# Linear attention with a routed MoE: order pinned in all wide tiles, weights in two transfers, a last turn over two PSUM tiles

## The chip, the cores and the metric

One core of a Trainium2 chip. The time is that of one execution on the device in microseconds; a median of three runs is given. Engines: PE (matmul), PEld (its weight loads), DVE, ACT, POOL, and SP, which only issues transfers.

## What is computed

Decayed linear attention over 4 batches, 8 heads, 768 positions, width 64, in blocks with a state that is carried on; its output as 3072 tokens of 512 goes through a mixture of eight experts, one per token:

```python
intra = einsum('bhij,bhjd->bhid', einsum('bhic,bhjc->bhij', qb, kb) * Dmask, vb)
inter = einsum('bhid,bhde->bhie', qb * lam_pow, kv_state)
out   = intra + inter
kv_state = lam_block * kv_state + einsum('bhsd,bhse->bhde', kb * rev_pow, vb)
...
logits = x @ w_gate + modality_bias[modality_id]
e_idx  = argmax(logits, axis=1)              # gate_w: its softmax weight
for e in range(8):
    out[e_idx == e] = gate_w * (relu(x @ w1[e]) @ w2[e])
```

## The kernel before

Attention runs over 24 blocks of 128 positions (`g`), two at a time in 12 pairs (`j`, the loop at L851). Per pair: scores on PE, masks on DVE, outputs from the state and from the masked scores on PE, a copy to `xt` on ACT. One pair later each block is turned into token rows together with its logits by `tokens`, in two halves (L291 to L300): PE writes PSUM, ACT copies to `xn`, and after the second half ACT's queue stores 128 rows to `xs` in device memory. The last pair has no later pair to hide in; its turn stands at L904 to L910, with a PSUM tile `xp` for each block whose halves it uses one after the other.

After every sixth block the tokens of a batch are routed (`route`, `ranks`, `places`), and one indirect write for each block fills a table `inv` (POOL) that lists tokens by expert; the last twelve come after attention, between the matmuls of tile 0. The MoE works through tiles of tokens of one expert: two wide tiles of 256 tokens from an early list (made from the first two batches, `early_list`, L439), two thin tiles (64 and 32 tokens), then ten or more wide ones from a late list (`late_list`). In this run 12 wide tiles are done and no conditional one.

A wide tile splits float32 operands into a high and a low part (`split`, L546: ACT casts `hi`, DVE subtracts for `lo`) and takes three matmuls for each product (`three`). The first layer (`wide`, L621) has four quarters of 24 matmuls of 256 columns; quarters 0 and 2 share one PSUM tile, 1 and 3 the other. After each quarter ACT makes `hh`, DVE makes `hl` (L632, L633) and `tail` splits a quarter of w2. Then the gathered rows of the next tile are transposed (`turn_rows`, L606), and the second layer (`second`) takes 48 matmuls of 512 columns. The weights of the next tile (`raw1` to `w1h`, `w1l`) are split too, each quarter once PE has read the old one. POOL gathers rows (`fetch_rows`, L573) and scatters results (L699); SP loads indices and weights (`fetch_w1` L588, `fetch_w2` L594, four transfers of 512 KB each, left out by a condition where the expert stays).

The order on an engine comes from a scheduler, except where `pinned` ties an operation behind the one pinned last on its engine. Before the change only the first wide tile is pinned (`run`, L950, third argument of `wide`), and most steps of the lists aren't.

Of the kernel before, what the change touches and what calls it, by code (L numbers as in the profile page):

```python
# [6 lines left out]
F32 = mybir.dt.float32  # L7
# [33 lines left out]
def linear_attention_moe(tc, qkv, lam, modality, wg, mbias, w1, w2, out):  # L41
    nc = tc.nc
    with ExitStack() as ctx:
# [159 lines left out]
        copies, logits, ranked, fades = [], [], [], []  # L203
# [77 lines left out]
        def outputs(g, pt, op):  # L281
            vt, blk = loaded(g)[2], g % HB
            for p in range(NP):
                for hl in range(2):
                    mm = pinned(nc.tensor.matmul(op[blk][halves2[hl ^ blk], p, :], vt[:, (2 * p + hl) * D : (2 * p + hl + 1) * D],  # L285
                                                 pt[:, hl, p, :], start=(g % NC == 0 and p == 0), stop=(p == NP - 1)))
            xt = work.tile([P, NP, P], F32, name="xt", bufs=3)
            copies.append(pinned(nc.scalar.copy(out=xt, in_=op[blk])))
            return xt, mm

        def tokens(g, hf, xt, xn, xp):  # L291
# [5 lines left out]
            copies.append(pinned(nc.scalar.copy(out=xn[:, blk, 2 * hf : 2 * hf + 2, :], in_=xp[:, :, : P + E])))  # L297
# [97 lines left out]

        def count_tiles(first, nm):
# [8 lines left out]
            nc.vector.tensor_tensor(out=ge, in0=cnt.unsqueeze(2).to_broadcast([1, E, CAP // TT]), in1=ge, op=ALU.is_ge)  # L405
            nt = const.tile([1, E], F32, name="nt" + nm)
            nc.vector.tensor_reduce(out=nt, in_=ge, axis=AX, op=ALU.add)
            return cnt, nt

        def list_ends(num, nm):  # L410
# [4 lines left out]
            nc.vector.tensor_tensor(out=tmp, in0=tri[:, :g, :g], in1=num.unsqueeze(1).to_broadcast([1, g, g]), op=ALU.mult)  # L415
            nc.vector.tensor_reduce(out=ends, in_=tmp, axis=AX, op=ALU.add)
            return ends

        def tile_list(num, delta, base0, items, nm, ends=None):
# [6 lines left out]
            pinned(nc.vector.tensor_tensor(out=past, in0=sidx[:, :items].unsqueeze(2).to_broadcast(sh),  # L426
                                           in1=ends.unsqueeze(1).to_broadcast(sh), op=ALU.is_ge))
            ex = const.tile([1, items], F32, name="ex" + nm)
            nc.vector.tensor_reduce(out=ex, in_=past, axis=AX, op=ALU.add)
            nc.vector.tensor_tensor(out=past, in0=past, in1=delta.unsqueeze(1).to_broadcast(sh), op=ALU.mult)  # L430
            at = const.tile([1, items], F32, name="at" + nm)
            nc.vector.tensor_reduce(out=at, in_=past, axis=AX, op=ALU.add)
            nc.vector.tensor_tensor(out=at, in0=at, in1=sidx[:, :items], op=ALU.add)
            if base0 is not None:
                nc.vector.tensor_tensor(out=at, in0=at, in1=base0.to_broadcast([1, items]), op=ALU.add)
            nc.vector.tensor_scalar(out=at, in0=at, scalar1=float(EMPTY), scalar2=None, op0=ALU.min)
            return ends, ex, at

        def early_list():  # L439
            cnt, full = count_tiles(TT, "A")  # L440
            ends = list_ends(full, "A")
            yield
# [9 lines left out]

            took = const.tile([1, E, EARLY], F32, name="took")
# [5 lines left out]
            yield ex, nA  # L459

        def late_list(cnt, n2, exA, nA):
# [9 lines left out]
            def first_of(those, nm):  # L471
# [25 lines left out]
            nc.vector.tensor_copy(out=exs[:, 0:1], in_=exA[:, EARLY - 1 : EARLY])  # L497
            others = const.tile([1, LIST], F32, name="others")
            facts = const.tile([1, 3, E], F32, name="facts")
            nc.vector.tensor_tensor(out=facts[:, 0, :], in0=sidx[:, :E], in1=exA[:, EARLY - 1 : EARLY].to_broadcast([1, E]),  # L500
                                    op=ALU.subtract)
# [4 lines left out]
            nc.vector.tensor_copy(out=start[:, 0, :], in_=exA[:, EARLY - 1 : EARLY])  # L506
# [15 lines left out]
            nc.vector.tensor_tensor(out=base[:, :E], in0=ebase, in1=nA, op=ALU.add)  # L522
# [71 lines left out]
        def fetch_w2(er, kw, after=None):  # L594
            for i in range(4):
                ld = nc.sync.dma_start(out=raw2[i], in_=w2[bass.ds(er, 1), :, 2 * i : 2 * i + 2].rearrange("o p f n -> p (o f) n"), **kw)
                if after is not None:
                    behind(ld, after)

        def turn_rows(cols, before=None, part=range(2), pin=False):  # L600
            for i in part:
                tp = ps.tile([P, 2, TT], F32, name=("x", "kv")[i], bufs=1)
                for j in range(2):
                    kc = 2 * i + j
                    for t, m in groups(cols):
                        mm = nc.tensor.transpose(out=tp[:, j, t * P : t * P + m],  # L606
                                                 in_=xg[t][:m, kc * (P + E) : kc * (P + E) + P], identity=ident[:m, :m])
                        if before is not None:
                            behind(mm, before, wait=False)
                        if pin and before is None:  # L610
                            pinned(mm)
                split(tp[:, :, :cols], xh[i][:, :, :cols], xl[i][:, :, :cols], pin)
# [118 lines left out]
        def fetch_both(er, kw):  # L731

            first, second = parts(F32)
            for i in range(4):
                nc.sync.dma_start(out=first[i], in_=w1[bass.ds(er, 1), :, i].rearrange("o p k f -> p (o k) f"), **kw)
            second = [t.rearrange("p k f -> p (k f)").rearrange("p (f n) -> p f n", f=2) for t in second]
            for i in range(4):
                nc.sync.dma_start(out=second[i],
                                  in_=w2[bass.ds(er, 1), :, 2 * i : 2 * i + 2].rearrange("o p f n -> p (o f) n"), **kw)
            return first, second  # L740

        raw1 = [const.tile([P, KC, TT], F32, name=f"raw1{i}") for i in range(4)]
        raw2 = [const.tile([P, 2, DM], F32, name=f"raw2{i}") for i in range(4)]
# [5 lines left out]
        w1h, w1l = parts(F32R)  # L749
# [15 lines left out]
        nums = const.tile([1, 1], I32, name="nums")  # L765
        thr = const.tile([1, E, CAP // TT], F32, name="thr")
# [84 lines left out]
        for j in range(1, pairs):  # L851
# [9 lines left out]
            if j == early + 1:  # L861
                exA, nA = next(listing)
# [20 lines left out]
            if j == early:  # L883
                listing = early_list()
                next(listing)
# [89 lines left out]
        def run_early(n):  # L975
# [3 lines left out]
            whole = wide(tail)  # L979
# [16 lines left out]
            w1h, w1l = parts(F32R)  # L996
# [11 lines left out]
        pins.clear()  # L1008
# [60 lines left out]
```

## Time and profile before

| | us |
|---|---|
| median of three runs (430.03 to 431.52) | 431.52 |
| the profiled execution | 429.08 |
| its span, first to last instruction | 427.4 |
| PE busy | 402.7 |
| DVE busy | 246.1 |
| ACT busy | 182.6 |
| POOL busy | 107.4 |
| mean granted TensorE clock, share of full | 0.986 |

Stages by PE's first matmul of each: attention to 109.2, tile 0 from 116.94, tile 1 from 141.66, thin tiles from 164.6, late wide tiles from 180.11 to 414.6, then the last result and the end at 427.4. A matmul record lasts longer than the step to the next one, since matmuls overlap: 0.28 us a record and some 0.12 us a step in the first layer.

### The profile page before, as it was taken

To read this page: it belongs to the slowest core of one execution; us is meant where nothing else is said; L and a number is where in the kernel's file an instruction comes from. 1 tells how busy PE (TensorE), PEld (TensorE's weight loads), DVE (VectorE), ACT (ScalarE), POOL (GpSimd) and SP (SyncE) were. 2 spreads that over 40 slices of the span, in tenths; PEclk is the share of its full clock that TensorE was granted. 3 is DMA by queue.
4 is the path that set the end of the run, shared out by engine and by line. 5 is a ranking of instruction groups with operands and counts; after the bars stand their busy time and mean duration, and the time that the engine had idled before them with its cause. 6 is when DMAs were issued, how large, how long until landed. Compare 5 with 4: busy or idle time off the path is not lost.

```text
span 427.4 us, 9911 instructions
## 1 busy us (share of the span) xinstructions
PE 402.7 (94%) x3864; PEld 356.8 (84%) x3864; DVE 246.1 (58%) x431; ACT 182.6 (43%) x277; POOL 107.4 (25%) x116
## 2 busy tenths in 40 slices
PE   8799999999599999899999999999999999999980
PEld 4599999899498986698989999898989899998960
DVE  4568777888389740377563819193755638191600
ACT  1032323324466331465554637182635546381510
POOL 5010144262268531154020111101020201101010
PEclk9899999999999999999999999999999999999995
DMA  5999999996830128412036684302020111101000
GB/s 202 324 357 348 391 381 342 348 327 216 277 129 3 51 64 281 170 55 78 26 78 221 212 284 147 135 20 78 26 78 25 54 49 46 50 2 41 11 30 18
DMA packets 25655, 63.85 MB, mean 149 GB/s; under 512 B 7157, under 2 KB 8701, under 8 KB 25600
## 3 DMA queue, kind: packets, MB, share of 16 engines
q1 hardware_dynamic: 17360, 43.36, 29.3%
q0 software_dynamic: 4768, 13.08, 9.2%
q10 hardware_dynamic: 3472, 6.69, 4.1%
q8 instruction: 32, 0.52, 0.5%
q14 instruction: 23, 0.19, 0.1%
HBM read 91.40 MB, written 14.07 MB: 247 GB/s over the span
## 4 chain that ended last, share of the span: by engine, by line
issue 48%; PE 20%; DMA 12%; POOL 8%; DVE 6%; SPq 2%; ACT 1%; POOLq 0%; ACTq 0%; DVEq 0%
PE s L232 5%; PE x L296 5%; PE o L285 5%; POOL out_dram L699 4%; DMA idx<-inv 4%; POOL xg L573 3%; DMA xg<-xs,idx 3%; PE o L278 3%; PE kv L252 2%; SPq L590 1%; DMA xg<-xs,idxA 1%; DMA raw<-in_w_dram 1%; DVE w1l L548 1%; DMA dk<-tab_d 1%; DVE w2l L548 1%
## 5 line engine op out<-in xcount | busy, mean ns | idle before, releaser
L615 PE MATMUL s<-xh,w1h 128*128 128x256 f32 x384 | 109.4, 285 | 0.7
L619 PE MATMUL s<-xh,w1l 128*128 128x256 f32 x384 | 107.9, 281 | 0.4 <-DVE w1l L548 0.4
L618 PE MATMUL s<-xl,w1h 128*128 128x256 f32 x384 | 107.8, 281 | 0.0
L548 DVE TENSOR_TENSOR w1l<-raw,w1h 128x1024 fp32r<-128x1024 f32 x46 | 55.6, 1225 | 84.4 <-ACT w1h L547 84.4
L615 PE MATMUL o<-w2h,hh 128*128 128x512 f32 x192 | 75.8, 395 | 0.0
L615 PEld LDWEIGHTS s<-xh,w1h 128*128 128x128 f32 x384 | 72.3, 188 | 4.0 <-DVE hl L633 2.3
L618 PE MATMUL o<-w2l,hh 128*128 128x512 f32 x192 | 74.8, 390 | 0.0
L619 PE MATMUL o<-w2h,hl 128*128 128x512 f32 x192 | 74.8, 389 | 0.0
L619 PEld LDWEIGHTS s<-xh,w1l 128*128 128x128 f32 x384 | 72.4, 188 | 0.6 <-DVE w1l L548 0.6
L618 PEld LDWEIGHTS s<-xl,w1h 128*128 128x128 f32 x384 | 72.4, 188 | 0.4
L548 DVE TENSOR_TENSOR w2l<-raw,w2h 128x1024 fp32r<-128x1024 f32 x48 | 58.4, 1216 | 2.6 <-ACT w2h L547 2.4
L547 ACT CAST w1h<-raw 128x1024 fp32r<-128x1024 f32 x46 | 47.5, 1053 | 27.3 <-PE s L618 21.3
L547 ACT CAST w2h<-raw 128x1024 fp32r<-128x1024 f32 x48 | 49.9, 1039 | 0.0
L699 POOL DMA_INDIRECT out_dram<-y,idx x20 | 20.2, 1008 | 106.7 <-ACT y L698 106.7
L698 ACT ACTIVATE y<-o,idx 128x512 f32<-128x512 f32 x20 | 13.8, 690 | 77.2 <-PE o L619 44.3
L573 POOL DMA_INDIRECT xg<-xs,idx x20 | 25.0, 1251 | 86.0 <-PE kv L606 74.8
L619 PEld LDWEIGHTS o<-w2h,hl 128*128 128x128 f32 x192 | 36.0, 188 | 7.7
L615 PEld LDWEIGHTS o<-w2h,hh 128*128 128x128 f32 x192 | 36.1, 188 | 7.2
L618 PEld LDWEIGHTS o<-w2l,hh 128*128 128x128 f32 x192 | 36.1, 188 | 7.1
L633 DVE SCALAR_TENSOR_TENSOR hl<-s,hh 128x512 fp32r<-128x512 f32 x48 | 32.8, 683 | 16.0 <-ACT hh L632 15.8
L388 POOL DMA_INDIRECT inv<-pay,sloti x24 | 32.5, 1356 | 25.2 <-PE x L296 6.3
L632 ACT ACTIVATE hh<-s 128x512 fp32r<-128x512 f32 x48 | 28.6, 595 | 21.9 <-PE s L619 20.6
(215 smaller groups left out, 473.8 us busy)
## 6 DMA issues: line engine op xcount, KB each, us to landing
raw<-in_w_dram SPq DMA_DIRECT2D x104, 512.0 KB
load<-in_qkv_dram SPq DMA_DIRECT2D x11, 2048.0 KB
xs<-xn ACTq DMA_DIRECT2D x24, 272.0 KB
load<-in_qkv_dram SPq DMA_DIRECT2D x4, 512.0 KB
w1h<-in_w_dram SPq DMA_DIRECT2D x4, 512.0 KB
w1l<-in_w_dram SPq DMA_DIRECT2D x4, 512.0 KB
dk<-tab_d SPq DMA_DIRECT2D x2, 256.0 KB
inv<-pad SPq DMA_DIRECT2D x2, 196.0 KB
```

Of the source, the lines that this page charges most:

```text
L232: pinned(nc.tensor.matmul(sp[:, hl, p, :], kt[r, p, :], qt[r, p, :], start=True, stop=True))
L285: mm = pinned(nc.tensor.matmul(op[blk][halves2[hl ^ blk], p, :], vt[:, (2 * p + hl) * D : (2 * p + hl + 1) * D], pt[:, hl, p, :], start=(g ...
L388: sc = nc.gpsimd.indirect_dma_start(out=inv, out_offset=bass.IndirectOffsetOnAxis(ap=at, axis=0), in_=pay[:, c, :], in_offset=None)
L547: cp = nc.scalar.copy(out=hi, in_=src)
L548: df = nc.vector.tensor_tensor(out=lo, in0=src, in1=hi.bitcast(F32), op=ALU.subtract)
L573: last = nc.gpsimd.indirect_dma_start(out=(to or xg)[t][:m], out_offset=None, in_=xs[:rows, :], in_offset=bass.IndirectOffsetOnAxis(ap=idx ...
L615: mm = pinned(nc.tensor.matmul(out, ah, bh, start=first, stop=False))
L618: pinned(nc.tensor.matmul(out, ah, bl, start=False, stop=False))
L619: return pinned(nc.tensor.matmul(out, al, bh, start=False, stop=last))
L632: act = nc.scalar.activation(out=hh[i], in_=hp, func=AF.Relu)
L633: low = nc.vector.scalar_tensor_tensor(out=hl[i], in0=hp, scalar=0.0, in1=hh[i].bitcast(F32), op0=ALU.max, op1=ALU.subtract)
L699: sc = nc.gpsimd.indirect_dma_start(out=out, out_offset=bass.IndirectOffsetOnAxis(ap=idx[:, t, 0:1], axis=0), in_=y, in_offset=None, bound ...
```

## The change

Seven edits:

- `wide` is pinned in all wide tiles, and so are the splits of the next rows and the next w1, which come in program order after the first layer.
- w1 and w2 are loaded in two transfers of 1 MB; `raw1`, `raw2`, `w1h` and `w1l` become one tile each, with four slices.
- In the last pair the halves of a block go to two PSUM tiles, the blocks to the two halves of each; DVE copies instead of ACT.
- The two transposition groups of tile 0 are parted: cast and subtraction of the first stand before the third turn, those of the second after it; w1[2] is split before the last logits and routing, w1[3] after.
- The early list is made in one piece, one pair earlier, and its steps are pinned; w1 of tile 0 is asked for a pair earlier.
- The load of w2 for tile 0 waits for a small memset that POOL does after it has issued the gather, not for the gather's landing.
- A few steps of the late list are pinned; the pins are cleared before each conditional tile.

```diff
         def tokens(g, hf, xt, xn, xp):
...
-            copies.append(pinned(nc.scalar.copy(out=xn[:, blk, 2 * hf : 2 * hf + 2, :], in_=xp[:, :, : P + E])))
+            cp = nc.scalar.copy if g < ng - HB else nc.vector.tensor_copy
+            pinned(cp(out=xn[:, blk, 2 * hf : 2 * hf + 2, :], in_=xp[:, :, : P + E]))
...
         def early_list():
             cnt, full = count_tiles(TT, "A")
             ends = list_ends(full, "A")
-            yield
...
-        def fetch_w1(er, kw, after=None):
-            for i in range(4):
-                ld = nc.sync.dma_start(out=raw1[i], in_=w1[bass.ds(er, 1), :, i].rearrange("o p k f -> p (o k) f"), **kw)
+        def fetch_halves(to, src, er, kw, after):
+            n = src.shape[2] // 2
+            for i in range(2):
+                ld = nc.sync.dma_start(out=to[:, 2 * i : 2 * i + 2].rearrange("p i a f -> p (i a f)"),
...
-            return [[work.tile([P, KC, TT], dt, name=f"{nm}{i}", bufs=1) for i in range(4)] for nm in ("w1h", "w1l")]
+            return [work.tile([P, 4, KC, TT], dt, name=nm, bufs=1) for nm in ("w1h", "w1l")]
...
+            if j == pairs - 1:
+                xp = [ps.tile([P, HB, 2, 256], F32, name="s", bufs=2) for _ in range(2)]
             for blk in range(HB):
-                if j == pairs - 1:
-                    xp = ps.tile([P, HB, 2, 256], F32, name="s", bufs=2)
...
-                    yield tokens(HB * j + blk, hf, xts[HB * j + blk], xns[j], xp[:, hf] if j == pairs - 1 else at)
+                    yield tokens(HB * j + blk, hf, xts[HB * j + blk], xns[j], xp[hf][:, blk] if j == pairs - 1 else at)
...
-            if j == early + 1:
+            if j == early:
                 er, _ = fetch_regs(listA, 0, True)
                 fetch_w1(er, {}, loads[-1])
             elif j == early + 2:
                 for i in range(EARLY):
                     fetch_idx(listA, i, idxA[i], after=loads[-1])
-                fetch_w2(er, {}, fetch_rows(idxA[0], TT, SOON * S, after=fades[-1]))
+                gathered = fetch_rows(idxA[0], TT, SOON * S, after=fades[-1])
+                asked = nc.gpsimd.memset(flag, 0)
+                behind(asked, gathered, wait=False)
+                fetch_w2(er, {}, asked)
...
         gated(pairs - 2)
-        turn_rows(TT, pin=True)
+        rows0 = turn_part(0, TT, pin=True)
+        split(*rows0)
+        rows1 = turn_part(1, TT, pin=True)
         next(turns)
+        split(*rows1)
         next(turns)
-        for i in range(2, 4):
-            split(raw1[i], w1h[i], w1l[i], True)
+        split(raw1[2], w1h[2], w1l[2], True)
         routed = gated(pairs - 1)
+        split(raw1[3], w1h[3], w1l[3], True)
...
-            turned = wide(first_tail if n == 0 else tail, before, n == 0)
+            turned = wide(first_tail if n == 0 else tail, before, True)
...
-                    turn_rows(TT, turned)
+                    turn_rows(TT, turned, pin=True)
...
-                        split(raw1[i], w1h[i], w1l[i])
+                        split(raw1[i], w1h[i], w1l[i], True)
...
-            whole = wide(tail)
+            whole = wide(tail, pin=True)
```

## Rows read from the trace of the kernel before

**Rows 1.** The page: busy time of PE (us, share of the span, instructions), and the clock line (the TensorE clock that was granted in each of 40 equal slices of the span, in tenths of full speed).

```profile
PE 402.7 (94%) x3864; PEld 356.8 (84%) x3864; DVE 246.1 (58%) x431; ACT 182.6 (43%) x277; POOL 107.4 (25%) x116
...
PEclk9899999999999999999999999999999999999995
```

**Rows 2.** Who PE waited for: us in total, how often, the longest.

```profile
PE s L296 <- ACT xn L297: 4.2, 2, 2.9
```

**Rows 3.** Windows by stage: from:to, length, then busy us (and instructions) of PE, PEld, DVE, ACT and POOL, granted clock, busy share of the DMA engines, GB/s.

```profile
109.00:117.00 8.00, 3.84 (x49) 2.80 (x45) 1.56 (x3) 3.30 (x8) 2.00 (x2) 1.00 0.84 287
...
127.00:142.00 15.00, 15.00 (x84) 13.09 (x84) 14.52 (x55) 7.88 (x11) 12.84 (x8) 1.00 0.02 3
...
251.00:274.50 23.50, 23.41 (x153) 21.32 (x153) 12.93 (x14) 12.28 (x16) 4.09 (x4) 1.00 0.61 211
```

**Rows 4.** Timeline of ACT at the end of attention: start, us, engine, line, operation, out<-in, shapes, count, and in brackets the idle time before it and what ended that. ACTq is a DMA issue on ACT's queue.

```profile
114.54 0.33 ACTq L299 DMA_DIRECT2D xs<-xn  x1
...
114.91 0.59 ACT L547 CAST xh<-x 128x512 fp32r<-128x512 f32 x1 [2.67 <-DMA raw<-in_w_dram]
```

**Rows 5.** Timeline of PE from the last turns of attention into the first wide tile.

```profile
109.21 0.63 PE L296 MATMUL s<-iw,xt 128*64 128x136 f32 x8
...
111.12 0.68 PE L296 MATMUL s<-iw,xt 128*64 128x136 f32 x8 [1.27 <-ACT xn L297]
...
111.73 0.66 PE L606 MATMUL x<-ident,xg 128*128 128x128 f32 x4
...
112.23 0.60 PE L606 MATMUL kv<-ident,xg 128*128 128x128 f32 x4
...
116.94 0.39 PE L615 MATMUL s<-xh,w1h 128*128 128x256 f32 x1
...
123.08 0.38 PE L615 MATMUL s<-xh,w1h 128*128 128x256 f32 x1
...
126.91 0.17 PE L400 MATMUL kv<-ohsum,onesb 128*128 128x8 bf16 x1 [0.73 <-DVE ohsum L375]
```

**Rows 6.** Timeline of POOL (second half of the gather for tile 0) and SP (issue of the four w2 loads).

```profile
106.35 1.00 POOL L573 DMA_INDIRECT xg<-xs,idxA  x1 [0.31 <-issue]
...
109.95 2.47 SPq L596 DMA_DIRECT2D raw<-in_w_dram  x4
```

**Rows 7.** Timeline of DVE: w1l[2] and w1l[3] of tile 0, the logits ahead of routing, hl of the first quarter right behind routing, and further on a copy out of PSUM.

```profile
118.42 2.36 DVE L548 TENSOR_TENSOR w1l<-raw,w1h 128x1024 fp32r<-128x1024 f32 x2 [1.60 <-ACT w1h L547]
...
120.70 0.27 DVE L304 TENSOR_REDUCE lg<-xn 128x16 f32<-128x64 f32 x1
...
122.34 0.68 DVE L633 SCALAR_TENSOR_TENSOR hl<-s,hh 128x512 fp32r<-128x512 f32 x1
...
153.60 0.42 DVE L729 COPY xf<-kv 128x256 f32<-128x256 f32 x1 [0.43 <-PE kv L728]
```

**Rows 8.** Timeline of DVE and PE in pair 8 and 9: state update, masks, and PE's last reader of these masks.

```profile
86.21 0.42 DVE L263 COPY state<-kv 128x256 f32<-128x256 f32 x1 [1.12 <-PE x L296]
...
86.95 2.36 DVE L239 TENSOR_TENSOR pt<-s,dk 128x1024 f32<-128x1024 f32 x2
...
90.60 1.04 PE L285 MATMUL o<-pt,load 128*64 128x128 f32 x16
```

**Rows 9.** Timeline of a steady wide tile at the end of the second quarter of its first layer, PE and DVE; the first and the last of eight tiles that show it (the others at 233.05, 256.60, 280.11, 303.63, 327.15 and 350.70).

```profile
208.01 1.23 DVE L548 TENSOR_TENSOR w1l<-raw,w1h 128x1024 fp32r<-128x1024 f32 x1 [8.19 <-ACT w1h L547]
...
209.16 0.68 DVE L633 SCALAR_TENSOR_TENSOR hl<-s,hh 128x512 fp32r<-128x512 f32 x1
...
209.57 0.28 PE L619 MATMUL s<-xh,w1l 128*128 128x256 f32 x1
...
209.89 0.39 PE L615 MATMUL s<-xh,w1h 128*128 128x256 f32 x1
...
374.20 0.28 PE L619 MATMUL s<-xh,w1l 128*128 128x256 f32 x1
...
374.56 0.39 PE L615 MATMUL s<-xh,w1h 128*128 128x256 f32 x1
```

**Rows 10.** Timeline of PE, POOL and SP from the end of a steady first layer to the start of the next: transpositions, first gather of the tile after next, issue of the w1 loads, first matmul.

```profile
239.24 0.60 PE L606 MATMUL x<-ident,xg 128*128 128x128 f32 x4
...
240.44 1.05 POOL L573 DMA_INDIRECT xg<-xs,idx  x1 [10.72 <-PE kv L606]
...
247.29 2.55 SPq L590 DMA_DIRECT2D raw<-in_w_dram  x4
...
251.04 0.28 PE L615 MATMUL s<-xh,w1h 128*128 128x256 f32 x1
```

**Rows 11.** Timeline of PE in the thin tiles and at the start of the wide tile behind them.

```profile
170.34 1.91 PE L650 MATMUL s<-w1h,xf 128*32 128x256 f32 x26 [0.55 <-DMA w1h<-in_w_dram]
...
178.18 2.00 PE L675 MATMUL o<-w1l,hnt 128*32 128x128 f32 x64
...
180.98 0.39 PE L619 MATMUL s<-xh,w1l 128*128 128x256 f32 x1 [0.37 <-DVE w1l L548]
```

**Rows 12.** Timeline of DVE and POOL between tile 0 and tile 1: four splits in a row, and a scatter of the index table.

```profile
134.08 4.61 DVE L548 TENSOR_TENSOR w1l<-raw,w1h 128x1024 fp32r<-128x1024 f32 x4
...
134.09 5.44 POOL L388 DMA_INDIRECT inv<-pay,sloti  x1 [0.30 <-issue]
```

**Rows 13.** The chain of work that ended last, in order of time (start, us, what): the load of w2 for tile 0.

```profile
109.95 4.52 DMA raw<-in_w_dram
```

More of the change, by code (lines that the diff above doesn't have):

```diff
@@ L201, in loaded @@
             return kt, qt, t[:, 2], t[:, 3]
-        copies, logits, ranked, fades = [], [], [], []
+        logits, ranked, fades = [], [], []
         def both(j, i):
@@ L287, in outputs @@
             xt = work.tile([P, NP, P], F32, name="xt", bufs=3)
-            copies.append(pinned(nc.scalar.copy(out=xt, in_=op[blk])))
+            pinned(nc.scalar.copy(out=xt, in_=op[blk]))
             return xt, mm
@@ L393, in write_slots, with chained @@
                     behind(sc, after)
+        chaining = [True]
+        def chained(op):
+            return pinned(op) if chaining[0] else op
         def count_tiles(first, nm):
@@ L458, in early_list @@
             pinned(nc.vector.tensor_reduce(out=nA, in_=took, axis=AX, op=ALU.add))
[L459 removed]
+            yield nA
         def late_list(cnt, n2, exA, nA):
@@ L505, in late_list @@
             start = const.tile([1, 3, 1], F32, name="start")
-            nc.vector.tensor_copy(out=start[:, 0, :], in_=exA[:, EARLY - 1 : EARLY])
+            pinned(nc.vector.tensor_copy(out=start[:, 0, :], in_=exA[:, EARLY - 1 : EARLY]))
             nc.vector.memset(start[:, 1, :], float(EMPTY))
@@ L521, in late_list @@
             nc.vector.memset(base[:, E:], 0.0)
-            nc.vector.tensor_tensor(out=base[:, :E], in0=ebase, in1=nA, op=ALU.add)
+            pinned(nc.vector.tensor_tensor(out=base[:, :E], in0=ebase, in1=nA, op=ALU.add))
             delta = per_expert("delta")
@@ L591, in fetch_w1 @@
                 if after is not None:
                     behind(ld, after, wait=after not in loads)
[L594 to L598, printed above, removed]
+        def fetch_w1(er, kw, after=None, to=None):
+            fetch_halves(raw1_all if to is None else to, w1, er, kw, after)
@@ new lines, in fetch_w2, with turn_part @@
+        def fetch_w2(er, kw, after=None, to=None):
+            fetch_halves(raw2_all if to is None else to, w2, er, kw, after)
+        def turn_part(i, cols, before=None, pin=False):
+            tp = ps.tile([P, 2, TT], F32, name=("x", "kv")[i], bufs=1)
+            for j in range(2):
+                kc = 2 * i + j
+                for t, m in groups(cols):
+                    mm = nc.tensor.transpose(out=tp[:, j, t * P : t * P + m],
+                                             in_=xg[t][:m, kc * (P + E) : kc * (P + E) + P], identity=ident[:m, :m])
+                    if before is not None:
+                        behind(mm, before, wait=False)
+                    elif pin:
+                        pinned(mm)
+            return tp[:, :, :cols], xh[i][:, :, :cols], xl[i][:, :, :cols], pin
@@ L600, in turn_rows @@
         def turn_rows(cols, before=None, part=range(2), pin=False):
             for i in part:
[L602 to L611, printed above, removed]
@@ L612, in turn_rows @@
-                split(tp[:, :, :cols], xh[i][:, :, :cols], xl[i][:, :, :cols], pin)
+                split(*turn_part(i, cols, before, pin))
         def three(out, ah, al, bh, bl, first, last, before=None):
@@ L733, in fetch_both, with quarters @@
             first, second = parts(F32)
[L734 to L743, printed above, removed]
+            second = second.rearrange("p i k f -> p i (k f)").rearrange("p i (f n) -> p i f n", f=2)
+            fetch_w1(er, kw, to=first)
+            fetch_w2(er, kw, to=second)
+            return quarters(first), quarters(second)
+        def quarters(t):
+            return [t[:, i] for i in range(4)]
+        raw1_all = const.tile([P, 4, KC, TT], F32, name="raw1")
+        raw2_all = const.tile([P, 4, 2, DM], F32, name="raw2")
+        raw1, raw2 = quarters(raw1_all), quarters(raw2_all)
         def parts(dt):
-            return [[work.tile([P, KC, TT], dt, name=f"{nm}{i}", bufs=1) for i in range(4)] for nm in ("w1h", "w1l")]
-        w1h, w1l = parts(F32R)
+            return [work.tile([P, 4, KC, TT], dt, name=nm, bufs=1) for nm in ("w1h", "w1l")]
+        w1h, w1l = (quarters(t) for t in parts(F32R))
         xg = [const.tile([m, ROW], F32, name=f"xg{t}") for t, m in groups(TT)]
@@ L861, in linear_attention_moe @@
             if j == early + 1:
-                exA, nA = next(listing)
+                nA = next(listing)
             if j == pairs - 1:
@@ L884, in linear_attention_moe @@
                 listing = early_list()
-                next(listing)
+                exA = next(listing)
+                chaining[0] = False
             xts[gs[1]], mm = outputs(gs[1], pts[1], op)
@@ L995, in run_early @@
             before = thin_second(idxs[EARLY + 1], hnt[1], both[1], FEW)
-            w1h, w1l = parts(F32R)
+            w1h, w1l = (quarters(t) for t in parts(F32R))
             for i in range(4):
```

34 lines of the change are left out of this document (19 added, 15 removed).

## The prediction

> **What bounds the kernel now.** I read the engine table and the clock line first [rows 1]: PE is busy for 94% of the span and its granted clock is nearly full in almost every slice, so time can come only from places where PE stands still, or from PE work that goes; the change takes no matmul away. The waits of PE come next: the largest is 4.2 us, in two waits of the token turn (L296) for ACT [rows 2]. The windows by stage place it [rows 3]: PE is busy for 3.84 of the 8 us from 109 to 117, between attention and the first expert tile, while a later wide tile shows 23.41 of 23.50. So that stage is one place to look. The other must be found in the timeline, since overlapping matmul records hide a stop that is shorter than one of them (0.28 us).
>
> The span is 427.4 us and the profiled run took 429.08, so 1.7 us lie around the span; the median of the timed runs is 431.52. I work out differences on the span and take them off the median.
>
> **Part 1, the turn at the end of attention.** Here PE and ACT hold each other up [rows 4, 5]. The second turn of block 22 starts at 111.12, though its input has been there since the first went out at 109.21: it writes the other half of the same PSUM tile and waits for ACT's copy of the first half. Then ACT stands until 114.54 ahead of the store of block 22, and the profile puts these 2.67 us down to the load of w2, which SP issued at 109.95 [rows 6]. The store needs nothing of those weights. My reading is that transfers share completion counters in turn and that the store's counter had last been the load's. Behind the store stand the two casts of xh (114.91) and the copy that frees the other PSUM tile, so that the first wide matmul starts at 116.94.
>
> The change does four things here. The halves of a block go to different PSUM tiles; their copies go to DVE; w2 is asked for once the gather has been issued (POOL is through with it at 107.35 [rows 6]) instead of once it has landed; and two weight transfers stand where four stood, so that the turn of the counters is another one and the store should meet a transfer that landed long ago. Worked forward from 109.21 with 0.50 us for a turn or a transposition (111.73 to 112.23): second turn 109.7, transpositions 110.2 and 110.7, third turn 111.2, fourth 111.7. DVE takes over four copies; the nearest row is a 128x256 copy out of PSUM at 0.42 [rows 7], so they are some 1.7 us. DVE's queue becomes: two copies to 110.8, logits, first xl from 111.55 (ACT's cast takes 0.59) to 112.2, third copy to 112.6, second xl to 113.2, fourth copy to 113.6. The wide tile needs the PSUM tile of the third copy: **112.7 instead of 116.94, 4.2 us earlier**.
>
> Does DVE then hold PE? Behind the fourth copy lie w1l[2], logits and routing, w1l[3] and the first hl in pinned order: 1.15 + 1.65 + 1.15 + 0.6 [rows 7], from 113.6 to 118.2. PE writes the PSUM tile that this hl reads again after two quarters and the ranks, 6.14 us after the start (116.94 to 123.08), at 118.8. It fits by 0.6. If ACT's queue has the store of block 23, which waits for the fourth copy, ahead of the cast of w1h[2], then w1l[2] starts at 115.4 and hl ends near 120: PE loses 1.1 there and 0.2 more before the count. The 0.73 us before the count (126.91) stays, or goes with a shift of DVE. So the gain lies between **2.9 and 4.7**; I take 4.2, as every row but the place of that store speaks for it. The gather now shares the DMA engines with w2 in its last microsecond; up to 1 us later is inside the lower end. The memset behind the gather has no row; if it took as long as the 1 us gather, w2 would still be asked for 1.6 us earlier than now, and w2 is first read after 115.5.
>
> The early list runs whole, one pair earlier: 14 short DVE steps come to stand ahead of a state update that now starts at 86.21 after DVE has been idle for 1.12 us [rows 8]. It would start some 0.75 later, and the masks behind it (86.95, 2.36 for two) would end at 90.05, while their last reader starts at 90.60. Cost nothing; that w1 is asked for 3 us earlier also brings nothing, as PE doesn't wait for it. Four steps of the late list go behind the w1 splits, up to 0.5 us on DVE, which also lies in the lower end.
>
> **Part 2, the steady tiles.** Here is what no list of waits names. Matmuls of the first layer follow each other by 0.12 us, but after the second quarter there is a gap, from 209.57 to 209.89 and so on in eight tiles to 374.20 and 374.56 [rows 9]. DVE shows why: it first splits the next tile's w1l (208.01), and then makes hl (209.16, ends at 209.84), and PE must wait for that before it writes the PSUM tile again. The gaps are 0.20 and then seven of 0.24 beyond the usual step, and the matmul behind each is 0.11 to 0.13 late as well: 0.31 + 7 x 0.37 = **2.9 us**. In the changed order hl and w2l of a quarter stand alone and the next w1l follows the first layer: hl is ready 1.3 us after its quarter (cast 0.6, hl 0.68), and PE wants it after 2.8. What do the splits meet in their new place? From the end of the first layer DVE has w2l until +2.9 (casts 0.6 and 1.05, then 1.2), two xl 1.3, four w1l 4.6: done at +8.8. The next first layer starts at +11.8 (239.24 to 251.04 [rows 10]). That cover is 3 us; without it each us is lost in each of eight tiles. Bounds 1.9 (the gaps without the late matmul) to 2.95. POOL's gathers now stand beside this burst; I take that at no cost and price it below.
>
> **Part 3, the thin tiles.** The merged w1l may be freed only as a whole: its next split then can't start before the last thin matmul has ended, 178.18 + 2.00, and ends 1.22 later; PE, which got it at 180.98, would get it at 181.5 [rows 11]. That is up to +0.5, and nothing if quarters are still freed singly. Against it, halved transfers save SP four issues on the way to the load on which PE waited for 0.55 until 170.34: up to -0.55. I take 0 for the two together, with +0.5 and -0.55 as ends.
>
> **Sum.** -4.2 - 2.9 + 0 = -7.1: span 420.3, profiled run 422.0, median **424.4 us**.
>
> **The rivals.** *The store goes on waiting for a weight load*, now another one: ACT stops until some 114.5 again and part 1 brings 0 to 0.5; part 2 is left, 428.6. For it: such a wait is in the rows, and who meets whom can't be read off them. Against it: the loads are fewer and earlier. 0.12. *The gap in the steady tiles stays*, because something else that reads this PSUM tile ends as late: 427.3. 0.06. *The thin stage gives part 1 back*: scatters, list, index and gather that feed the thin tiles run on POOL and SP, and PE has no slack there (170.34). If that chain keeps its own pace, all but 1 us of the 4.2 is lost: 427.6. For it: POOL is busy for 12.84 of the 15 us from 127 to 142 [rows 3]. Against it: its scatters start on PE's first quarter, which comes earlier by the same. 0.07.
>
> *Slower: POOL held by the splits.* One scatter took 5.44 us (134.09 [rows 12]), beside four w1l back to back on DVE; the change puts such a burst beside both gathers of each steady tile (1.05 us at 240.44 now). The next w1 load waits for the gather's landing, until 247.29, which is +8 on the clock of part 2 [rows 10]. With two holds of 4.4 us it would go out at +17 and, as 2 MB took 4.52 us [rows 13], land at +21.5, before its split at +26: hidden. The rival decides from a lateness of 13.5 us on. If each gather were held for 8.3 us, 3 us would be lost in eight tiles: 431.5 - 4.2 - 2.9 + 24 = 448. The Trainium skill (SBUF — State Buffer, Who interferes with whom) says that a DVE instruction with two SBUF inputs contends with a GpSimd instruction that reads SBUF, and that the later one waits in full; the 5.44 us agree, the gathers of 1.05 us beside single w1l splits do not. The rows bear out one hold for a burst and no more, so 0.04.
>
> **How the numbers follow.** The forecast has 0.71, and its own range is 423.3 to 427.2 (gains of 4.7 + 2.95 + 0.55, and of 2.9 + 1.9 - 0.5). Below, the range takes in 1.3 for the scatter of a median (the runs lie between 430.03 and 431.52); above, it has to reach to the three cases near 428 to leave no more than 2 in 10 out: 422.0 to 429.0. About 0.5% (2.2 us) can be told from no change. Faster: the forecast and most of the three rivals that keep 2.9 us or more, 0.88. Same: what is eaten of those three, 0.08. Slower: 0.04.
>
> **What would show it.** Right: a first wide matmul near 112.7, with ACT not stopped ahead of a store; no gap at a third quarter, and steady tiles of 23.15 us (11.4 + 11.75) where they were 23.52; the w1l splits in a row under the second layer. Wrong: ACT waiting for a weight load again; PE waiting at L650 for more than 1 us; gathers longer than 5 us with PE waiting at L606.

## The result, and the profile after

The changed kernel takes **419.01 us** (median of 4 runs, 418.13 to 420.79) beside 431.47 of the kernel before in the same call: ratio 0.972, 95% interval 0.969 to 0.976, faster. The gain of 12.5 us is larger than the 7.1 forecast, and the time lies below the range. Medians and ratios, here and below, are of fast runs alone, those at most 1.5% above the fastest of their kernel. In four later calls, each on one chip, the two medians were 6.7, 8.0, 9.8 and 5.4 us apart. The mean of the five is 8.5 us, so part of the 12.5 belongs to that call and part to the change.

The profiled run of the changed kernel took 420.79 with a span of 419.0. Its clock line, in forty slices, answers to [rows 1]:

```profile
PEclk9999999999899999999999999999999999999995
```

Its waits of PE (engine, line, waited for: us in total, times, longest) answer to [rows 2]:

```profile
PE kv L252 <- DVE kd L212: 2.6, 1, 2.6
PE x L614 <- DMA xg<-xs,idxA: 1.9, 1, 1.9
...
PE s L631 <- DVE w1l L554: 1.0, 1, 1.0
```

The 4.2 us of L296 for ACT are gone from the list. A wait of 1.9 us for the gathered rows of tile 0 is new, and the eleventh slice of the clock is an 8. The timeline of the turn shows what became of [rows 4 to 6], first ACT with its DMA issues:

```profile
110.36 0.59 ACT L553 CAST xh<-x 128x512 fp32r<-128x512 f32 x1 [3.41 <-PE x L614]
110.42 0.33 ACTq L300 DMA_DIRECT2D xs<-xn  x1
```

On PE, from the first two turns to the first wide matmul:

```profile
106.34 1.10 PE L296 MATMUL s<-iw,xt 128*64 128x136 f32 x16
107.37 0.33 PE L614 MATMUL x<-ident,xg 128*128 128x128 f32 x1
109.62 0.70 PE L614 MATMUL x<-ident,xg 128*128 128x128 f32 x3 [1.92 <-DMA xg<-xs,idxA]
110.11 1.06 PE L614 MATMUL kv<-ident,xg 128*128 128x128 f32 x4
111.10 2.08 PE L296 MATMUL s<-iw,xt 128*64 128x136 f32 x16
113.11 0.45 PE L627 MATMUL s<-xh,w1h 128*128 128x256 f32 x1
```

On POOL, the second half of the gather for tile 0 and the memset behind it:

```profile
103.06 1.00 POOL L579 DMA_INDIRECT xg<-xs,idxA  x1 [0.31 <-issue]
104.06 0.09 POOL L919 MEMSET flag<- 1x1 int32 x1
```

On SP, the load of w2 from its first transfer on (three transfers in one row, its two among them):

```profile
104.18 3.07 SPq L597 DMA_DIRECT2D raw<-in_w_dram  x3
```

The first two turns run as one row of 16 matmuls, and the store goes out right behind the first cast: ACT no longer stops ahead of it. w2 is asked for at 104.18, while the gather is still on its way; the gathered rows arrive at 109.6. Behind this wait four transpositions take 1.06 us, where [rows 5] have 0.60: the granted clock is 0.50 from 110 to 113, so PE runs at the lower of its two levels, 1.2 and 2.4 GHz. The windows (columns as in [rows 3]) give 0.80 as the mean of the stage, and a steady tile as 23.10 us where it was 23.50:

```profile
105.00:113.00 8.00, 6.08 (x68) 5.13 (x64) 4.44 (x8) 3.81 (x8) 1.46 (x2) 0.80 0.97 346
...
244.85:267.95 23.10, 23.10 (x154) 21.20 (x152) 13.40 (x14) 12.28 (x16) 5.43 (x4) 1.00 0.63 221
```

At the third quarter of a steady tile the matmuls now follow each other by 0.12 us as everywhere else, where [rows 9] have steps of 0.32 to 0.36:

```profile
204.18 0.28 PE L631 MATMUL s<-xh,w1l 128*128 128x256 f32 x1
204.30 0.28 PE L627 MATMUL s<-xh,w1h 128*128 128x256 f32 x1
204.42 0.28 PE L630 MATMUL s<-xl,w1h 128*128 128x256 f32 x1
```

On DVE, hl of that quarter now stands alone, and the four splits for the next tile come in a row under the second layer:

```profile
205.19 0.69 DVE L645 SCALAR_TENSOR_TENSOR hl<-s,hh 128x512 fp32r<-128x512 f32 x1 [0.67 <-ACT hh L644]
...
214.06 4.62 DVE L554 TENSOR_TENSOR w1l<-raw,w1h 128x1024 fp32r<-128x1024 f32 x4
```

A wait list can't be added up here, so I measured each stage from one start of PE to the next, in the traces of both kernels (us; "again" are e10 and e8 below):

| stage | before | before again | after | after again |
|---|---|---|---|---|
| scores of the last pair to the first turn of block 22 | 7.94 | 7.77 | 6.93 | 6.93 |
| from there to the first wide matmul ("the turn") | 7.73 | 7.60 | 6.77 | 5.29 |
| to the second layer of tile 0 | 13.71 | 13.69 | 13.29 | 13.39 |
| to the second layer of tile 1 | 22.85 | 22.84 | 22.79 | 22.79 |
| to the tile behind the thin ones | 26.61 | 26.90 | 25.41 | 25.42 |
| that tile | 23.90 | 23.91 | 24.05 | 24.46 |
| eight steady tiles | 188.13 | 188.10 | 184.82 | 184.82 |

In three more traces of the changed kernel, without the wait for the gather, the second row reads 3.62, 3.63 and 3.65, and the first 7.91, 7.99 and 7.73. So the first row is no gain of the change: 5 of all 18 traces have 6.93 (the first and e8 here, and e5, e6 and e7), the other 13 have 7.73 to 8.16, in both kernels. In e4 PE stops there in the middle of a row, with no engine named:

```profile
105.21 0.93 PE L285 MATMUL o<-pt,load 128*64 128x128 f32 x13 [0.43 <-issue]
```

With nothing for the first row and 3.63 for the second, the table adds up to 4.0 + 0.35 + 0.05 + 1.35 - 0.35 + 3.3 = 8.7 us, near the mean of 8.5.

### The profile page after: what moved, and what is told of

Read it like the earlier page. It is cut to its first block, busy times and chain, and to the rows that moved or that the text cites. A ratio compares the mean times of both kernels' runs of the same rounds, so it can differ in the third digit from the quotient of the medians.

```text
span 419.0 us, 9681 instructions
## 1 busy us (share of the span) xinstructions
PE 396.8 (95%) x3864; PEld 354.4 (85%) x3864; DVE 252.6 (60%) x435; ACT 181.3 (43%) x273; POOL 114.4 (27%) x117
## 4 chain that ended last, share of the span: by engine, by line
issue 44%; POOL 9%; DMA 8%; SPq 2%; DVE 0%; POOLq 0%
POOL out_dram L711 6%; DMA idx<-inv 4%; DMA xg<-xs,idx 4%; POOL xg L579 3%; SPq L567 1%; SPq L597 1%; POOL out_dram L695 0%; SPq L564 0%; POOLq L579 0%; POOLq L711 0%; DVE ats L538 0%; DVE listB L540 0%; DVE atB L438 0%; SPq L569 0%; DVE listB L541 0%
## 5 line engine op out<-in xcount | busy, mean ns | idle before, releaser
L627 PE MATMUL s<-xh,w1h 128*128 128x256 f32 x384 | 108.1, 281 | 0.0
L631 PEld LDWEIGHTS s<-xh,w1l 128*128 128x128 f32 x384 | 73.5, 191 | 1.2 <-DVE w1l L554 1.2
L711 POOL DMA_INDIRECT out_dram<-y,idx x20 | 28.1, 1403 | 98.2 <-ACT y L710 93.8
L554 DVE TENSOR_TENSOR w1l<-raw,w1h 128x1024 fp32r<-128x1024 f32 x46 | 53.4, 1219 | 0.9 <-PE o L687 0.8
L553 ACT CAST w1h<-raw 128x1024 fp32r<-128x1024 f32 x46 | 45.1, 1065 | 0.0
```

Of the source, the lines that this page charges most:

```text
L553: cp = nc.scalar.copy(out=hi, in_=src)
L554: df = nc.vector.tensor_tensor(out=lo, in0=src, in1=hi.bitcast(F32), op=ALU.subtract)
L627: mm = pinned(nc.tensor.matmul(out, ah, bh, start=first, stop=False))
L631: return pinned(nc.tensor.matmul(out, al, bh, start=False, stop=last))
L711: sc = nc.gpsimd.indirect_dma_start(out=out, out_offset=bass.IndirectOffsetOnAxis(ap=idx[:, t, 0:1], axis=0), in_=y, in_offset=None, bound ...
```

## The experiments

Theory: each part of the change brings what its own stage lost, and the sum falls short because single terms were read too small. Rival: something that no stage of one trace shows (the clock, the chip, the order of all at once) makes the difference.

**Both kernels again** (r1, e10 the kernel before; r2, e4, e8, e12 the changed one; no edit).

> The kernel before, unchanged, for a second trace. Theory A (my sum, with a start that differs from run to run): the time before the first pair's second scores differs between executions, the granted clock at 14 to 20 us was 0.72 in one trace and 1.00 in the other; then a second trace has the same 23.5 us tiles and the same stop of ACT ahead of the store, and its span differs from 427.4 only in the first 25 us, by up to 2 us. Theory B (something else in the timed runs is slower than in the first trace): the second trace shows longer stops later, in the turn or in the thin tiles. Ratio to itself 1.000 within 0.4%.

> The changed kernel, unchanged, for a second trace: its timed runs had spans of 416.4 to 417.3 where the first trace had 419.0. Theory A: the 2 us lie in the wait for the gathered rows at the turn (1.92 us in the first trace) and in the first split after the thin tiles (1.13 us), which depend on when transfers land. Theory B: they lie in the first 25 us.

> The changed kernel as it is, once more, beside the three others. Theory (the terms stand side by side: 4.2 to 4.4 at the turn, 0.41 in each of ten tiles, up to 1 in the thin stage): 8.5 to 9.5 us below the kernel before, ratio 0.978 to 0.980. Rival (the shorter stop at the turn also spares PE a fall of its clock, which the sum of terms doesn't hold): 10.5 to 12.5 us, ratio 0.971 to 0.976, with a granted clock of 1.0 through the turn here and below 0.9 in what keeps the long stop.

> The changed kernel as it is, on a third chip. Theory (sum of the terms by the traces so far: 4.4 at the turn, 3.4 in eight tiles, up to 1 in the thin stage): 8 to 9.5 us below the median of the kernel before, ratio 0.978 to 0.982; the 12.5 of the first call hold 3 to 4 us that are not the change's. Rival (the change's gain is 12 us and the two later calls fell short by chance): ratio 0.970 to 0.974 again.

> The kernel before as it is, one more trace. Theory A: ACT's stop of 2.0 to 2.7 us ahead of the store, 15.5 to 16 us from the last scores to the first wide matmul, and a granted clock below 0.9 in the 8 us behind it. Theory B: the same stop, the clock at 1.0.

> The changed kernel as it is, beside them. Theory: 8.9 us of the stages and 1 to 1.5 of the clock make 10 us, ratio 0.976 to 0.978. Rival: 12.5 us, 0.971.

Measured: r1 429.88 (ratio 1.000, 0.993 to 1.007); r2 423.90 (0.988, 0.981 to 0.996); e4 422.47 (0.981, 0.974 to 0.988); e8 420.59 (0.977, 0.973 to 0.982); e10 428.46, one run; e12 423.73 (0.987, 0.981 to 0.993). The steady tiles keep their 23.10 against 23.52 everywhere. What differs between executions lies for the most part ahead of them: a late start, the 1 us ahead of the turn, a late gather, a fall of the clock, and a stop of ACT in tile 0. The 12.5 of the first call didn't come again.

**Pins alone and the changed kernel without them** (r3, r4).

```
-            turned = wide(first_tail if n == 0 else tail, before, n == 0)
+            turned = wide(first_tail if n == 0 else tail, before, True)
...
-                    turn_rows(TT, turned)
+                    turn_rows(TT, turned, pin=True)
...
-                        split(raw1[i], w1h[i], w1l[i])
+                        split(raw1[i], w1h[i], w1l[i], True)
...
-            whole = wide(tail)
+            whole = wide(tail, pin=True)
...
```

> The kernel before with the pins of the wide tiles alone (order in all wide tiles, next rows and next w1 split under the second layer), four transfers, old turn. Theory A: eight gaps of 0.37 us go, 2.9 to 3.4 us faster, 428 us, ratio 0.993; everything ahead of the late wide tiles as before. Rival: the pins also bring the thin tiles forward or cost there, and the ratio lies at 0.985 or at 1.0.

> The changed kernel without the pins in tiles 1 and later. Theory A: it loses the 2.9 to 3.4 us of the steady tiles and stands at 422.3, ratio 0.979. Rival (the pins are worth more, because tile 1 and the thin stage hang on them too): it loses 5 us or more, ratio 0.984 or above.

r3 is this edit on the kernel before, r4 takes it out of the changed one. Measured: r3 424.46 (0.989, 0.983 to 0.994), r4 424.73 (0.989, 0.982 to 0.996). A steady tile takes 23.14 us in r3 and 23.42 in r4, where it is 23.52 before and 23.10 changed. So the pins alone bring 0.38 of the 0.41 of part 2; without them the rest of the change brings 0.1.

**The turn, taken apart** (e1, e5, e6 on the kernel before; e2 on the changed one). e1 has the order of the turn and the earlier w2, e5 the order alone, e6 the earlier w2 alone; e2 undoes the earlier w2 in the changed kernel.

```
+                asked = nc.gpsimd.memset(flag, 0)
+                behind(asked, gathered, wait=False)
-                fetch_w2(er, {}, gathered)
+                fetch_w2(er, {}, asked)
```

> The kernel before with part 1 alone, without its early list: the halves of a block in two PSUM tiles, their copies on DVE, the second pair of transpositions and splits behind the third turn, and w2 asked for once the gather is issued. No pins in the wide tiles, four transfers a weight. Theory (the terms stand side by side, and each keeps its own size): from the scores of the last pair to the first wide matmul 11.5 to 12 us where the kernel before has 15.7 to 15.9, steady tiles of 23.52 as before, the time 4 to 4.5 us shorter, ratio 0.990. Rival 1 (the store goes on waiting for a weight load, as four transfers still follow each other): ACT stops ahead of the store by 2 us or more, the turn takes 14.5 to 15.9 us, gain 0 to 1.5. Rival 2 (the thin stage gives the turn's gain back): the turn is short, but from the second layer of tile 1 to the first tile behind the thin ones it takes 3 us longer, ratio 0.998.

> The kernel before with the order of the turn alone: two PSUM tiles for the halves, copies on DVE, second transpositions and splits behind the third turn. w2 is asked for once the gather has landed, in four transfers, as before. Theory A (the order takes ACT's stop away, with either timing of w2): no stop of ACT of 2 us ahead of the store or the casts, from the scores of the last pair to the first wide matmul 11.5 to 12 us, the time 4 to 4.5 us below the kernel before. Theory B (either half of the cure is enough for the store: the earlier w2 or the fewer transfers; with neither it meets a weight load): ACT stops ahead of the store by 2 to 3 us, the turn takes 13.5 to 15 us, gain 1 to 2.5.

> The kernel before with w2 alone asked for once the gather is issued; one PSUM tile for the halves of a block, copies on ACT, transpositions and splits where they were. Theory A (the order is what counts): ACT stops ahead of the store as before by 2.7 us, the turn takes 15.5 us or more, time that of the kernel before. Theory B (the store waited because the load was issued just ahead of it): no stop of ACT, the turn is 2.5 to 2.9 us shorter, 13 us, and the time with it.

> The changed kernel with one line undone: w2 is asked for once the gather has landed, as before, instead of once it is issued. Theory A (the order and the PSUM tiles took the stop away; what is shared with the load costs at most a late gather): no stop of ACT ahead of the store, the turn takes 11.5 us, PE never waits for the gathered rows, time the same as the changed kernel, or up to 2 us shorter in those executions in which the gather came late there. Theory B (the stop went because w2 is asked for earlier, so that the store meets a transfer that has landed): ACT stops ahead of the store again by 2 to 3 us and the first wide matmul is 2 to 4 us later, time 2 to 4 us longer.

Measured: e1 425.30 (0.988, 0.982 to 0.994), e5 430.24 (0.998, 0.995 to 1.002), e6 425.03 (0.988, 0.985 to 0.992), e2 425.95 (0.986, 0.980 to 0.993). ACT at the turn in e5:

```profile
113.69 0.33 ACTq L300 DMA_DIRECT2D xs<-xn  x1
114.06 0.59 ACT L548 CAST xh<-kv 128x512 fp32r<-128x512 f32 x1 [4.39 <-DMA raw<-in_w_dram]
```

And in e6:

```profile
109.39 0.33 ACTq L299 DMA_DIRECT2D xs<-xn  x1
109.75 0.59 ACT L547 CAST xh<-x 128x512 fp32r<-128x512 f32 x1 [1.65 <-PE s L296]
```

With the new order alone the stop is still there, longer (4.39 us). The turn, counted from the first turn of block 22 as in the table, takes 4.26 us, but PE meets the stop behind the first wide matmuls: 2.9 us of waiting for xh. With the earlier w2 alone the stop is gone, and the turn takes 6.31; with both it takes 3.68 (e1). So at the turn some 1.4 us come from when w2 is asked for and, on top of it, 2.6 from the order, which brings nothing by itself: from the first turn to the second layer of tile 0 e5 takes 22.9 us, the kernel before 21.3 and 21.4. This split rests on one trace of each; by the medians e6 gains 5.3 us and e1 5.2, which is more than the turn holds in e6 and can't show what the order adds. Theory A of e5 and e6 falls.

In e2, with w2 late, two transfers and the new order, the stop doesn't come back: the turn takes 3.60 and PE doesn't wait for the gather. The store goes out 2.7 us after the load was issued; [rows 13] have 4.52 for such a load to land:

```profile
109.56 1.94 SPq L597 DMA_DIRECT2D raw<-in_w_dram  x3
112.25 0.33 ACTq L300 DMA_DIRECT2D xs<-xn  x1
```

The longer time of e2 lies elsewhere in its trace, in scores of pair 2 that start 2.8 us later than e4's and a clock of 0.75 and 0.83 at 128 to 136.

Which transfer the store waits for can be read off the instruction records in the traces: a transfer counts up a numbered semaphore when it lands, and ACT waits for that of the store just ahead of issuing it. In the kernel before that wait ends at 114.49, and the load of [rows 13] at 114.47. In all nine traces with four transfers a weight, of both kernels, the store of block 22 and the first transfer of w2 have the same semaphore, 108. In all nine with two, w2 has 106 and 107 and the store 102. So with four transfers the store stops if w2 has not landed (before, r1, r3, e5, e9, e10) and passes if it was asked for early enough (e1, e3, e6); with two it doesn't wait for w2, whenever that comes (e2).

**Four transfers** (e3, on the changed kernel) **and half tiles** (e11).

```
-            n = src.shape[2] // 2
-            for i in range(2):
+            n = src.shape[2] // 4
+            for i in range(4):
```

e11 instead makes w1h and w1l of two tiles each, with half of the slices in each ([P, 2, KC, TT]), and has keep_busy(24) for keep_busy(20) at the start.

> The changed kernel with four transfers for each weight instead of two; the tiles stay merged. Theory A (two transfers matter only to the thin stage): the turn is the one of the changed kernel, PE waits for w1h's load in the thin stage again by 0.5 to 0.9 us, from the second layer of tile 1 to the tile behind the thin ones 26.1 to 26.6 us instead of 25.4 to 26.1, time 0.5 us longer, no difference that can be told. Theory B (the number of transfers decides whom the store meets): ACT stops ahead of the store or ahead of the casts by 2 us or more, time 2 to 4 us longer.

> The changed kernel with two half tiles of w1h and of w1l instead of one whole tile each, and with 24 instead of 20 idle matmuls at the start. Theory A (what a merged tile costs the thin stage is its release as a whole): PE's wait for w1l behind the thin tiles falls from 1.0 us to 0.4, the first tile behind them starts 0.5 us earlier on the clock of tile 1's second layer, and the scores of pair 2 start at 22 us or earlier; time 0.5 to 1 us below the changed kernel, ratio 0.975 to 0.976. Theory B (that wait is DVE's own pace): it stays 1.0, time as the changed kernel.

Measured: e3 424.48 (0.989, 0.984 to 0.993): no stop of ACT, 11.49 us from the scores to the first wide matmul, and the way to the tile behind the thin ones is 26.55 us, where the five traces of the changed kernel have 25.41 to 26.09. e11 422.65 (0.983, 0.977 to 0.989). PE's wait for w1l behind the thin tiles, in e8:

```profile
176.86 0.38 PE L631 MATMUL s<-xh,w1l 128*128 128x256 f32 x1 [0.97 <-DVE w1l L554]
```

And in e11:

```profile
179.66 0.39 PE L632 MATMUL s<-xh,w1l 128*128 128x256 f32 x1 [0.31 <-DVE w1l L554]
```

0.97 becomes 0.31, and the tile behind the thin ones takes 23.38 instead of 24.02 to 24.46. With four transfers into merged tiles the wait stays (0.94 in e3). So the merged tile is what makes PE wait there. The median is 1.1 below that of e12 beside it, which these runs can't tell from nothing.

**PE kept busy** (e7, the changed kernel with 4 more idle matmuls at the start; e9, the kernel before with idle matmuls in the two waits of the turn).

```
-        keep_busy(20)
+        keep_busy(24)
```
```
         next(turns)
+        keep_busy(4)
         next(turns)
...
         next(turns)
+        keep_busy(11)
         next(turns)
```

> The changed kernel with 24 instead of 20 idle matmuls after the tables at the start, ahead of the first state update. Theory (a late start of that update, at 16.1 us or later, goes with a granted clock of 0.6 from 16 to 20 us and costs some 2 us, in either kernel, whichever execution it falls on; it is scatter that no term of the change holds): with PE busy up to 15.4 us the clock stays at 1.0, the scores of pair 2 start near 21.3 us in every trace, and the time is up to 1 us below the changed kernel's. Rival (the late executions are late because their loads are late, and the clock adds nothing): scores of pair 2 between 21 and 23.5 us as before, time as the changed kernel or 0.3 longer.

> The kernel before with 4 idle matmuls behind the first and 11 behind the third turn of the last pair, where PE stood for 1.3 and 2.9 us; ACT's stop ahead of the store stays. Theory A (the long stop of PE makes the granted clock fall, and that fall is the term that the sum doesn't hold): clock 1.0 from the first wide matmul on in the trace, 6.1 us from it to the ranks instead of 7.4, and the time 1 to 1.5 us below the kernel before, ratio 0.9965 to 0.9975. Theory B (the falls are scatter that comes whatever PE does): the clock falls behind the turn as often as before, the time that of the kernel before or 0.3 us above.

Measured: e7 420.27 (0.978, 0.974 to 0.981) beside 420.59 of e8: no difference in time, though its trace has the clock at 1.00 from 16 to 24 us and the scores of pair 2 at 21.84. e9 428.41 (0.999, 0.994 to 1.003): the clock stays at 1.00 behind the turn, but in e10 it does so too, without the idle matmuls. Windows of r1, behind the same stop:

```profile
112.00:116.00 4.00, 1.40 (x11) 1.22 (x12) 1.29 (x2) 2.04 (x5) 1.23 (x2) 0.89 1.03 417
116.00:120.00 4.00, 4.00 (x27) 4.00 (x26) 3.17 (x7) 1.77 (x3) 0.00 (x0) 0.68 0.79 311
```

The fall costs r1 1.3 us (7.45 from the first wide matmul to the third quarter, 6.14 in [rows 5]). It stands behind the stop in r1, r3 and e5, and not in the first trace, nor in e10. That the stop makes it is not settled.

## Why the prediction was right in direction and too small

Two steps failed. The sum took part 3 at 0, and it brought 1.0; and the range gave 1.3 us to scatter, where medians of the changed kernel lie 4.9 apart. The second put the time outside the range.

**Part 1: the mechanism is shown, and the size nearly right.** Forecast 4.2, measured 4.0 without a late gather; the forecast had 3.49 us from 109.21 to the first wide matmul, three traces have 3.62 to 3.65. The cause named there, that the store of block 22 stood behind w2's load, holds: asking for w2 earlier alone takes the stop away (e6), the order alone doesn't (e5). What I had not weighed is that the store escapes with either half of the cure: the earlier load (e1, e3, e6) or two transfers (e2). The shared counter, there only a reading, is in the records: semaphore 108 for both. The first wide matmul came at 113.11, not 112.7, for another reason than feared, and although the turn began 2.9 us earlier than in [rows 5] (a start without the delay, and the shorter first row of the table): the gather, to which I gave up to 1 us, landed late by 1.9 in the first trace (where the fall of the clock behind it made up most of another 1.2), by 1.5 in e8 and 1.7 in e11, and in time in r2, e4 and e12. The memset took 0.09 us.

**Tile 0: mis-sized.** I left the 0.73 before the count where it was, and it stayed (0.75). But tile 0's way to its second layer became 0.3 to 0.4 shorter, most of it ahead of that: the third quarter starts 5.83 and 5.92 us after the first matmul, where it was 6.14 and 6.13.

**Part 2: right, and a little small.** 2.9 forecast, 3.3 measured: 0.41 in each of eight tiles, where I had added up single gaps to 0.37. The splits' cover held, and PE waits for none of them in the steady tiles. The pins are what brings it (r3).

**Part 3: the step that failed.** I took 0 with ends of +0.5 and -0.55, and these were read off waits. The loss at the end, +0.5, came (0.97 instead of 0.37, the tile 0.15 to 0.55 longer). The gain on the load was not 0.55 but 1.15, because the wait of [rows 11] holds only the time in which the list shows PE idle. PE in the thin first layer of e10, the kernel before again:

```profile
168.13 0.63 PE L650 MATMUL s<-w1h,xf 128*32 128x256 f32 x6
169.60 1.91 PE L650 MATMUL s<-w1h,xf 128*32 128x256 f32 x26 [0.83 <-DMA w1h<-in_w_dram]
171.44 0.65 PE L661 MATMUL kv<-ident,hn 128*128 128x128 f32 x4
```

The same in the changed kernel:

```profile
164.85 1.93 PE L662 MATMUL s<-w1h,xf 128*32 128x256 f32 x32
166.72 0.66 PE L673 MATMUL kv<-ident,hn 128*128 128x128 f32 x4
```

From the first of 32 matmuls to the next transposition it is 1.87 us now; in e10 it was 3.31, and 3.02 in the first trace of before (169.16 to 172.18). The stops were 1.44 and 1.15, of which 0.83 and 0.55 are listed. That is the reading that part 2 had warned of: overlapping records hide a stop. Over all runs, nine traces with four transfers have 2.35 to 3.89 (e3 2.91), and of nine with two, seven have 1.87, and e12 and r2 have 2.41 and 2.50, with no wait listed at all. Net of the loss, part 3 brought 1.35 - 0.35 = 1.0.

**The range: scatter mis-sized.** I allowed 1.3 us below for the spread of medians, from three runs within 1.5 us. Later calls have single runs of the kernel before anywhere from 426.5 to 437.4, two outliers aside, and medians of the changed kernel from 419.0 to 423.9. The terms as measured, 8.7 us, would have put the time at 422.8, inside the range; the other 3.8 us of that call are not explained by a stage of the change, and where they come from stays open.

**The rivals.** The store that goes on waiting: not in the changed kernel. The steady gap that stays: no. The thin stage that gives the gain back: no, it got shorter. POOL held by the splits: the gathers took 1.22 us in the mean (1.25 before) and started ahead of the burst, not beside it. The scatters of y met it:

```profile
217.52 2.06 POOL L711 DMA_INDIRECT out_dram<-y,idx  x1 [3.68 <-ACT y L710]
```

The burst ends at 218.68, this scatter 0.9 later, and the mean of the scatters rose from 1.01 to 1.40 us. By the Trainium skill (SBUF — State Buffer, Who interferes with whom), that the later one waits in full, it would end 1.0 after the burst, so here the trace agrees; nobody waits for it. The gathers of 1.05 us, which I had held against this rule, don't speak against it: they started no later than the split beside them, while four gathers of the kernel before that started up to 0.15 us behind a split (183.22 to 196.40) took 1.94 to 2.06.

## What to carry to other kernels

Measure a stop from start to start of PE's rows against the same work elsewhere; a list of waits shows only what overlapping records leave over, and here it halved one term and hid another. A store can stop its engine for an unrelated load on another queue, when both count on the same semaphore; here an earlier load freed it, and so did a number of transfers that gave the store another semaphore, while reordering the stopped engine's work only moved the place where the stop is met. Count a stage from the point where the change begins: here a stop of 1 us ahead of it came in some executions and not in others. And before you set a range from three close runs, look in several traces for what differs between executions of one kernel.

## What the runs showed of the hardware beside that

**A stop of ACT that belongs to no kernel.** In 9 of 18 traces ACT stands ahead of the third hh of tile 0, and the profile names only something remote. In r2:

```profile
122.70 0.60 ACT L644 ACTIVATE hh<-s 128x512 fp32r<-128x512 f32 x1 [4.46 <-remote]
```

It makes PE wait 1.8 to 2.2 us for cntB, and in the changed kernel tile 0's way to its second layer takes 15.8 to 16.0 us instead of 13.3 to 13.4. The kernel before has it in r1 and not in e10, the changed one in r2, e4 and e12 and not in the first trace and e8. The medians of the changed kernel fall the same way: 423.9, 422.5 and 423.7 in the calls whose trace has it, 419.0 and 420.6 in the others. The same three traces have the 1 us more ahead of the turn. But the medians of the kernel before don't follow: 430.6, 430.5, 430.4 and 429.1 in the four later calls. So that these stops make the calls differ is not shown; only one execution of each was traced, and where they come from stays open.

**Two levels at the start.** In 5 of 18 traces, of either kernel, the granted clock is 0.57 to 0.67 from 16 to 20 us, and the scores of pair 2 start at 23.1 to 23.9 us instead of 20.9 to 22.3. PE had stood for 1.8 to 2.4 us ahead of its first state update there. The length of that wait alone doesn't decide: in four other traces it was 2.3 to 3.3 us, and the clock stayed at 1.00. Nor does a late update, which e7 took for a sign: in e10 and e12 it starts at 16.56 and 16.35, as late as there. The first trace of the kernel before has the late start and that of the changed one doesn't: 1.9 of the 8.4 us between them.
